# Batch 0 of a sketched attention reworked (token-major k, z from k kᵀ, squares as features), and W1 three waves ahead of W2 at the end

## The chip, the core and the metric

One core of a Trainium2 chip runs the kernel. Its engines have a queue of instructions each and wait for one another by semaphores: TensorE (PE; its weight loads are shown apart as PEld), VectorE (DVE), ScalarE (ACT), GpSimd (POOL), and SyncE (SP), which here only issues DMAs. The metric is the time of one execution on the device in microseconds (us). A profile gives one execution with the start and length of each instruction.

## What is computed

```
a = S1 x,  b = S2 x              # x is a row of q or k (32 numbers), S1 and S2 are 8 x 32
phi(x)[8 i + j] = a[i] b[j]      # 64 features of a row
kv  = sum over tokens of phi(k)^T v          # 64 x 32, for each batch and head
z   = sum over tokens of phi(k)              # 64
x   = (phi(q) kv) / (phi(q) z + 1e-6)        # heads side by side: 128 numbers per token
h   = x w_in                                 # 128 -> 2048
out = (h / (1 + exp(-beta h))) w_out         # 2048 -> 128
```

There are 4 batches, 4 heads and 1088 tokens in a batch, so 4352 tokens reach the second half. All arrays are float32. The kernel folds beta into w_in (winp) and 1/beta into w_out (woutp), both in float16, so that a plain Silu stands between the two products.

## The kernel before

The order of the work on all five engines is written out by hand. Tokens lie across partitions by head: partition 32h + i of a loaded tile holds 34 consecutive tokens of head h. A transpose on VectorE turns 32x32 blocks.

The second half runs in *waves*. `w1` (L320) multiplies up to 512 tokens of xT by two 128-column blocks of winp into one of two PSUM buffers called wave (two banks each), and ScalarE takes the Silu of 1024 columns into g (L338). `w2` (L297) multiplies g by woutp and accumulates over sixteen blocks in the one buffer moeout; after the last block VectorE transposes it into o_sb (L314), which SP stores. Tokens are cut as 256, 256, seven times 512, and 256: 68 waves. In the first, second and last cut a wave is four blocks of 256 tokens. `first` issues a W1 if its tokens are there, `second` issues the oldest outstanding W2, and `rest` (L355) runs what is left when the attention is done: W2 of the wave before goes ahead of the next W1.

The other PSUM buffers are "two" (two banks) and "one" (one bank), a single buffer each, so whoever takes one waits until its last reader is done.

Batch 0 stands in straight code ahead of the waves (L656 to L708). k is transposed (`turn_k`), projected by S1 and S2 with features on partitions (`kps`) and transposed back (`kab`). `gram` multiplies the projections to get z (with `gram_terms` and `gram_z`), `outer` forms phi(k) on VectorE, `kv` sums phi(k)ᵀ v on PE. For q, `spread` makes a and b for all 64 features on partitions, `asb` copies a to SBUF on ScalarE, `mult` multiplies b by it; `den0`, `invert`, `spread_rc`, `num0` and `divide0` write xT. The first 512 tokens go in this stage, the other 576 in the waves' stage. `beta_half` spreads beta over the partitions by two matmuls and a copy, POOL makes winp in eight pieces, and ScalarE makes woutp in sixteen.

From there on one list of names, SEQ (L807), gives the order in which the steps are issued. W and V are `first` and `second`. For batch 1: tk1, kp1, ka1 transpose, project and transpose back k; tq1, qp1, qa1 do it for q; o and O are `outer` for k on POOL and on VectorE, p and P for q; t1n transposes phi(q); Z1 sums phi(k); va1 and vb1 are `kv`; np1, nz1, d1, i1, n1, x10, x11 make z, kv, the denominators, their inverses, the numerators and xT. For the rest of batch 0 they are aB, c0, c1, bB, mB, dB, iB, nB, xB.

Loads are issued on SP in the order k0, q0 (first part), v0, half of w_in, half of w_out, q0 (rest), k1, the other halves, q1, v1, k2, q2, v2; beta and S2 on ACT's queue, S1 and beta_jp on POOL's. Thirteen matmuls on constants run at the start and four before the first W1 (`keep_warm`).

Of the kernel before, what the change touches and what calls it, by code (L numbers as in the profile page):

```python
# [14 lines left out]
P = 128  # L15
# [3 lines left out]
def kernel(  # L19
# [31 lines left out]
    q_chk = [(0, 8), (16, 9)]  # L51
    QW = 32 * 9

# [3 lines left out]
    WARM0 = 13  # L57

    tok_chk = [(0, 256), (256, 256)]
    tok_chk += [(o, min(TCH, NTOK - o)) for o in range(512, NTOK, TCH)]  # L60
# [7 lines left out]
    pso = ctx.enter_context(tc.tile_pool(name="pso", bufs=1, space=bass.MemoryType.PSUM))  # L68
    ps2 = ctx.enter_context(tc.tile_pool(name="ps2", bufs=1, space=bass.MemoryType.PSUM))
    ps1 = ctx.enter_context(tc.tile_pool(name="ps1", bufs=1, space=bass.MemoryType.PSUM))  # L70
# [16 lines left out]
    def cut(t, ap, extra=0):  # L87
# [6 lines left out]
    w_out_sb = sb([P, NJ, P], F32, "w_out_sb")  # L94
    idle = sb([P, P], F16, "idle")
    nc.vector.memset(idle, 1.0)  # L96
    nc.scalar.dma_start(
        out=bass.AP(
            tensor=beta4.tensor,
            offset=beta4.offset,  # L100
            ap=[[32 * beta4.ap[0][0], 4], [1, DFF // 4]],
        ),
        in_=moe_beta.rearrange("(r c) -> r c", r=4),
    )
    sr = []
    for n, (s_, eng) in enumerate(((S1, nc.gpsimd), (S2, nc.scalar))):
        t = sb([P, D], F32, f"sr{n}")
        eng.dma_start(
            out=t, in_=bass.AP(tensor=s_.tensor, offset=s_.offset, ap=[[0, P // R], [D, R], [1, D]])
        )  # L110
        sr.append(t)
    nc.gpsimd.dma_start(out=beta_jp, in_=moe_beta.rearrange("(j p) -> j p", p=P))
    k_t, q_t, v_t = {}, {}, {}

    def load_rows(src, dst, b, tag, parts=((0, T),)):
        if b not in dst:
            dst[b] = ld.tile([P, T, D], F32, tag=tag, name=tag)
# [9 lines left out]


    def load_v(b):
        t = v_t[b] = ld.tile([P, H, NJK, D], F32, tag="v", name="v")  # L130
        if b < B - 1:
            for h in range(H):
                nc.sync.dma_start(
                    out=t[:, h],
                    in_=bass.AP(
                        tensor=v.tensor, offset=v[b, h].offset, ap=[[NJK * D, 4], [T * D, 32], [1, NJK * D]]
                    ),
                )
            return
# [14 lines left out]

    def load_wout(j0, j1):
        nc.sync.dma_start(
            out=w_out_sb[:, j0:j1, :],
            in_=moe_w_out[j0 * P : j1 * P, :].rearrange("(j p) m -> p j m", p=P),
        )

    K_PARTS = ((0, 18), (18, T))
    QA0 = 2 * q_chk[0][1]
    load_rows(k, k_t, 0, "k", K_PARTS)
    load_rows(q, q_t, 0, "q", ((0, QA0),))
    load_v(0)
    load_win(0, DFF // 2)
    load_wout(0, NJ // 2)
    load_rows(q, q_t, 0, "q", ((QA0, T),))
    load_rows(k, k_t, 1, "k")
    load_win(DFF // 2, DFF)  # L170
    load_wout(NJ // 2, NJ)
    load_rows(q, q_t, 1, "q")
# [6 lines left out]
    def keep_warm(n):  # L179
        t = pso.tile([P, TCH], F32, tag="moeout", name="warm")  # L180
        for _ in range(n):
            nc.tensor.matmul(out=t, lhsT=idle, rhs=cut(idle, [[0, 4], [1, P]]), start=True, stop=True)  # L182

    ones = sb([P, P], F32, "ones")
# [3 lines left out]
    ident = sb([P, P], F32, "ident")  # L188
    make_identity(nc, ident)

    hm = sb([P, 2, R], F32, "hm")
    nc.vector.memset(hm, 0.0)
    for h in range(H):
        nc.vector.memset(hm[32 * h : 32 * h + 32, h % 2, :], 1.0)
    gm = sb([P, 4], F32, "gm")
    nc.vector.memset(gm, 0.0)
    for c in range(4):
        nc.vector.memset(gm[32 * c : 32 * c + 32, c : c + 1], 1.0)
    e3 = sb([P, 3], F32, "e3")
    nc.vector.memset(e3, 0.0)  # L200
    nc.vector.memset(e3[:, 1:2], 1.0)

    mk = sb([P, H, R], F32, "mk")
    nc.gpsimd.tensor_tensor(
        out=mk,
        in0=cut(ident, [[2 * R, H], [1, R]]),
        in1=cut(ident, [[2 * R, H], [1, R]], 64),
        op=mybir.AluOpType.add,
    )

    kT2, qT2 = [], []
    for n in range(2):
        qT2.append(sb([P, T, 32], F32, f"qT{n}"))
# [106 lines left out]
    def w1():  # L320
# [22 lines left out]
        if j0 + jn == NJ:  # L343
            moe["ci"] += 1
            moe["w"] = 0
# [502 lines left out]
```

## Time and profile before

| | |
|---|---|
| median of three runs | 116.13 us (115.93 to 116.38) |
| span of the profiled execution, first to last instruction | 113.9 us |
| mean granted TensorE clock | 0.967 |
| PE, DVE, ACT, POOL busy | 100.8, 74.2, 79.2, 28.8 us |
| Silu, L338 | 68 x 1022 ns |
| W1, L329, and W2, L304 | 160 matmuls each |
| first write into xT done | 19.54 us |
| kv of batch 1 begins on PE | 35.5 us |
| last W2 done | 109.9 us |

The profile's own time is its span of 113.9 us; the device time of a run is taken around the whole execution and is about 2.2 us more. Busy PE time is modelled and overlaps, so "busy" is not peak. A float32 matmul appears as two records, and each has a weight load. The granted clock is the share of its full clock that TensorE was allowed.

### The profile page before, as it was taken

The numbers are of one execution on the slowest core, as the hardware profiler recorded it, in microseconds if no ns is written. First come the engines' busy times: TensorE is split into PE (matmuls) and PEld (weight loads), VectorE is DVE, ScalarE is ACT, GpSimd is POOL, SyncE is SP. The second block draws the span as 40 slices with busy tenths as digits, with TensorE's granted clock in tenths as the row PEclk, the third lists the DMA queues.
The fourth block names the chain that finished last, engine by engine and source line by source line (L and its number), as shares of the span: only waits on it lengthen the run. The fifth ranks groups of instructions, "written<-read, shape, count | busy, mean of one in ns | idle before, by whom it ended". The sixth has DMA issues, their size and how long they took to land.

```text
span 113.9 us, 2875 instructions
## 1 busy us (share of the span) xinstructions
PE 100.8 (89%) x1169; PEld 48.3 (42%) x1169; DVE 74.2 (65%) x133; ACT 79.2 (70%) x100; POOL 28.8 (25%) x40
## 2 busy tenths in 40 slices
PE   6969998877999999999999999999998899799840
PEld 2235463323784533435553343465343333334620
DVE  3386828596999799899998899999587001100210
ACT  1426157959879853898996469999926889898830
POOL 6500082807970000530840035065000000000000
PEclk9999558999999999999999999999999999999998
DMA  3679998287234200038502462300320500140323
GB/s 101 233 170 268 307 348 289 106 245 210 103 104 115 53 17 0 3 60 214 211 5 36 75 182 45 53 0 0 60 38 0 84 9 0 26 66 9 50 42 46
DMA packets 24436, 11.33 MB, mean 100 GB/s; under 512 B 18756, under 2 KB 22884, under 8 KB 24424
## 3 DMA queue, kind: packets, MB, share of 16 engines
q1 hardware_dynamic: 23664, 11.05, 37.3%
q8 instruction: 9, 0.15, 0.6%
q10 hardware_dynamic: 696, 0.09, 0.5%
q0 software_dynamic: 64, 0.02, 0.1%
q14 instruction: 3, 0.02, 0.1%
HBM read 8.93 MB, written 2.23 MB: 98 GB/s over the span
## 4 chain that ended last, share of the span: by engine, by line
PE 70%; ACT 12%; DVE 7%; DMA 3%; issue 2%; ACTq 1%; POOL 0%; DVEq 0%
PE moeout L304 24%; PE wave L329 22%; ACT g L338 11%; PE kvz L476 5%; DMA sr<-in_S_dram 3%; PE dps L622 3%; PE betaps L246 3%; PE nps L636 3%; DVE o_sb L314 2%; PE kps L392 2%; PE ndps L545 2%; PE bps L452 1%; DVE xT L647 1%; PE nps L580 1%; PE qps L392 1%
## 5 line engine op out<-in xcount | busy, mean ns | idle before, releaser
L338 ACT ACTIVATE g<-wave 128x1024 f16<-128x1024 f32 x68 | 66.2, 1022 | 18.3 <-PE wave L329 18.3
L304 PE MATMUL moeout<-g,woutp 128*128 128x512 f16 (+1 forms) x160 | 37.8, 347 | 3.5 <-ACT g L338 2.3
L329 PE MATMUL wave<-xT,winp 128*128 128x512 f16 (+1 forms) x160 | 39.7, 347 | 1.2 <-ACT g L338 1.1
L304 PEld LDWEIGHTS <-woutp 128*128 128x128 f16 x160 | 14.9, 97 | 20.8 <-issue 7.8
L329 PEld LDWEIGHTS <-winp 128*128 128x128 f16 x160 | 14.8, 97 | 17.6 <-issue 6.3
L314 DVE STREAM_TRANSPOSE o_sb<-moeout 128x512 f32<-128x512 f32 (+1 forms) x10 | 6.3, 627 | 21.4 <-PE moeout L304 21.2
L428 POOL TENSOR_TENSOR qo<-qab 128x512 f32<-128x512 f32 (+1 forms) x8 | 12.1, 1539 | 10.7 <-DVE qab L413 10.7
L428 POOL TENSOR_TENSOR kp<-kab 128x512 f32<-128x512 f32 (+1 forms) x6 | 7.2, 1216 | 25.7 <-PE wave L329 22.6
L439 DVE STREAM_TRANSPOSE qt<-qo 128x512 f32<-128x512 f32 (+1 forms) x12 | 8.7, 750 | 0.0
L428 DVE TENSOR_TENSOR kp<-kab 128x512 f32<-128x512 f32 (+2 forms) x10 | 8.6, 883 | 0.0
L476 PEld LDWEIGHTS kvz<-kp,v 128*32 128x32 f32 x288 | 5.3, 125 | 4.1 <-issue 3.7
L476 PE MATMUL kvz<-kp,v 128*32 128x64 f32 x288 | 6.4, 244 | 0.0
L182 PE MATMUL warm<-idle 128*128 128x512 f16 x17 | 5.5, 481 | 1.1 <-DVE idle L96 1.1
L256 POOL TENSOR_TENSOR winp<-w_in_sb,beta_bc 128x256 f16<-128x256 f32 x8 | 5.6, 728 | 2.7 <-DMA w_in_sb<-in_moe_w_in_dram 2.7
L365 DVE STREAM_TRANSPOSE kT<-k 128x1088 f32<-128x1088 f32 (+2 forms) x5 | 5.3, 1057 | 1.2 <-DMA k<-in_k_dram 1.2
L572 DVE STREAM_TRANSPOSE rb<-rc 128x576 f32<-128x576 f32 (+1 forms) x9 | 5.9, 685 | 0.2
L271 ACT ACTIVATE woutp<-w_out_sb,rbeta 128x128 f16<-128x128 f32 x16 | 5.1, 394 | 1.1 <-DMA w_out_sb<-in_moe_w_out_dram 1.1
L562 DVE STREAM_TRANSPOSE dT<-dps 128x288 f32<-128x288 f32 (+1 forms) x5 | 2.4, 474 | 4.4 <-PE dps L551 2.4
L371 DVE STREAM_TRANSPOSE qT<-q 128x1088 f32<-128x1088 f32 (+2 forms) x5 | 5.2, 1049 | 0.0
L647 DVE TENSOR_TENSOR xT<-nps,rb 128x576 f16<-128x576 f32 x6 | 4.5, 744 | 0.6 <-PE nps L636 0.3
L392 PE MATMUL kps<-kT,sk 64*32 64x288 f32 x64 | 3.1, 415 | 1.9 <-DVE qp L469 1.0
L428 DVE TENSOR_TENSOR qo<-qab 128x512 f32<-128x512 f32 x4 | 4.8, 1234 | 0.1
(75 smaller groups left out, 77.6 us busy)
## 6 DMA issues: line engine op xcount, KB each, us to landing
v<-in_v_dram SPq DMA_DIRECT2D x15, 144.0 KB
k<-in_k_dram SPq DMA_DIRECT2D x3, 544.0 KB, 8.6
q<-in_q_dram SPq DMA_DIRECT2D x3, 544.0 KB
w_in_sb<-in_moe_w_in_dram SPq DMA_DIRECT2D x2, 512.0 KB
w_out_sb<-in_moe_w_out_dram SPq DMA_DIRECT2D x2, 512.0 KB
out_dram<-o_sb SPq DMA_DIRECT2D x16, 64.0 KB, 2.0
out_dram<-o_sb SPq DMA_DIRECT2D x10, 32.0 KB, 5.6
k<-in_k_dram SPq DMA_DIRECT2D x1, 288.0 KB
```

What stands on the lines that cost most here:

```text
L182: nc.tensor.matmul(out=t, lhsT=idle, rhs=cut(idle, [[0, 4], [1, P]]), start=True, stop=True)
L256: (eng or nc.gpsimd).tensor_tensor(out=winp[:, c0:c1], in0=w_in_sb[:, c0:c1], in1=beta_bc[:, c0:c1], op=MUL)
L304: nc.tensor.matmul(out=moe["acc"][:, :tw], lhsT=woutp[:, j, :], rhs=g[jj], start=(j == 0), stop=(j == NJ - 1),)
L314: nc.vector.transpose(out=o_sb[:, :nt, :].rearrange("p t d -> p (t d)"), in_=moe["acc"][:, :tw])
L329: nc.tensor.matmul(out=wv[:, jj // per, o : o + tw], lhsT=winp[:, (j0 + jj) * P : (j0 + jj + 1) * P], rhs=xT[:, t0 : t0 + tw], start=True, ...
L338: nc.scalar.activation(out=g[:, :, :gw], in_=wv[:, :, :gw], func=ACTF.Silu)
L392: nc.tensor.matmul(out=t[32 * g : 32 * g + 32, pi, :JW], lhsT=skc[rows, :], rhs=moving(rows, g), start=True, stop=True,)
L428: (eng or nc.vector).tensor_tensor(out=cut(dst[b][:, j0:j1], [[F, n], [R, R], [1, R]]), in0=cut(a0, [[2 * R, n], [1, R], [0, R]]), in1=cut ...
L439: nc.vector.transpose(out=QT[b][:, j0:j1].rearrange("p j h c s -> p (j h c s)"), in_=QO[b][:, j0:j1].rearrange("p j h f -> p (j h f)"),)
L476: nc.tensor.matmul(out=KVZ[b][32 * h : 32 * h + 32, :F], lhsT=v_t[b][:, h, j, :], rhs=KP[b][:, j, h, :], start=(j == 0), stop=(j == NJK - ...
L572: nc.vector.transpose(out=rb, in_=cut(rc, [[1, n * tn], [0, 32]], i * tn))
L647: nc.vector.tensor_tensor(out=cut(x0, [[32 * (QB[2 * i + 1] - QB[2 * i]), 2], [1, JW]]), in0=t[:, :, :JW], in1=rb, op=MUL,)
```

## The change

The kernel after differs in three places.

*Batch 0, k.* k0 is loaded in two pieces of tokens j = 0..4 and 5..8 of each group of nine, padded to 36. `kab0` multiplies transposed k as the stationary operand by a block-diagonal S, which gives token-major projections at once; ScalarE copies them and `outer0` multiplies PSUM by the copy on VectorE, or copy by copy on POOL. z comes from k kᵀ: `kk` sums k kᵀ over tokens on PE (68 matmuls), `kk_s2` multiplies by S2, `z_terms` by S1, `z_sum` sums and spreads.

*Batch 0, q.* 4 a b = (a + b)² - (a - b)². `spread_sq` makes the 64 sums and 64 differences of a head for 256 tokens in one matmul, ScalarE squares them (`square`), and z and kv carry the factors 1/4 and -1/4. The first 256 tokens are finished ahead of the first wave; the next 256 are steps dA, iA, nA, xA in SEQ after the first W; the last 576 go as before. S1 is loaded on ACT's queue and S2 on SP's between the two k pieces. v is loaded by token group for all batches (32 partitions a piece, all heads), with a POOL memset before each. Half of beta is spread by DMA, and POOL makes the first half of winp; the second half is a product on VectorE from PSUM (bC, wC0, wC1). woutp is made in four products, two on VectorE (w0, w1) and two on POOL (u2, u3). There are five warming matmuls.

*The end.* The first 512 tokens are one cut, with their first four waves of 256 tokens; the last cut of 256 tokens has eight waves of two blocks, so there are 72 waves. `rest` issues W1 first and W2 when three waves are outstanding, and odd cuts there accumulate in the buffer "one".

```diff
-    WARM0 = 13
-
-    tok_chk = [(0, 256), (256, 256)]
-    tok_chk += [(o, min(TCH, NTOK - o)) for o in range(512, NTOK, TCH)]
+    WARM0 = 5
...
-    K_PARTS = ((0, 18), (18, T))
-    QA0 = 2 * q_chk[0][1]
-    load_rows(k, k_t, 0, "k", K_PARTS)
-    load_rows(q, q_t, 0, "q", ((0, QA0),))
+    load_k0(0, NJ0)
+    load_s(1, S2, nc.sync)
+    load_k0(NJ0, NJK)
+    load_rows(q, q_t, 0, "q", ((0, NA),))
     load_v(0)
-    load_win(0, DFF // 2)
+    load_win(0, DFF // 4)
+    load_beta(0, 512)
+    load_win(DFF // 4, DFF // 2)
+    load_beta(512, 1024)
     load_wout(0, NJ // 2)
-    load_rows(q, q_t, 0, "q", ((QA0, T),))
-    load_rows(k, k_t, 1, "k")
+    load_rows(q, q_t, 0, "q", ((NA, T),))
     load_win(DFF // 2, DFF)
     load_wout(NJ // 2, NJ)
+    load_rows(k, k_t, 1, "k")
     load_rows(q, q_t, 1, "q")
     load_v(1)
...
+    def spread_s():
+        t = bank(2, "srep")
+        nc.tensor.matmul(
+            out=t[:, : 2 * R],
+            lhsT=s12.rearrange("p h d -> p (h d)"),
+            rhs=ident[: 2 * R, : 2 * R],
+            is_transpose=True,
+            start=True,
+            stop=True,
+        )
+        nc.scalar.copy(out=st.rearrange("p n r -> p (n r)"), in_=t[:, : 2 * R])
+        ADD, SUB = mybir.AluOpType.add, mybir.AluOpType.subtract
+        nc.gpsimd.tensor_tensor(
+            out=sbd, in0=cut(st, [[0, H], [1, 2 * R]]), in1=cut(gm, [[1, H], [0, 2 * R]]), op=MUL
+        )
+        for n, op in enumerate((ADD, SUB)):
+            nc.gpsimd.tensor_tensor(
+                out=spm[:, n], in0=cut(st, [[1, R], [0, R]]), in1=cut(st, [[0, R], [1, R]], R), op=op
+            )
...
+    def prep_wout(j0, j1, eng):
+        scaled.update(range(j0, j1))
+        eng.tensor_tensor(
+            out=woutp[:, j0:j1, :],
+            in0=w_out_sb[:, j0:j1, :],
+            in1=cut(rbeta[:, j0:j1], [[1, j1 - j0], [0, P]]),
+            op=MUL,
         )
...
+    waves = []
+    for ci, (t0, tw) in enumerate(tok_chk):
+        if ci == 0:
+            lst = [(0, 256, 0, 4), (0, 256, 4, 4), (256, 256, 0, 4), (256, 256, 4, 4)]
+            lst += [(0, TCH, j, 2) for j in range(8, NJ, 2)]
+        else:
+            lst = [(0, tw, j, 2) for j in range(0, NJ, 2)]
+        for n, (o, w, j0, jn) in enumerate(lst):
+            waves.append((ci, t0, o, w, j0, jn, n == 0, n == len(lst) - 1))
...
+    def w2(wave, g):
+        ci, t0, o, w, j0, jn, head, tail = wave
+        tw = tok_chk[ci][1]
+        if head:
+            if moe["free"] and ci % 2:
+                moe["acc"] = ps1.tile([P, TCH], F32, tag="one", name="moeout1")
+            else:
+                moe["acc"] = pso.tile([P, TCH], F32, tag="moeout", name="moeout")
...
             nc.tensor.matmul(
-                out=moe["acc"][:, :tw],
-                lhsT=woutp[:, j, :],
+                out=moe["acc"][:, o : o + w],
+                lhsT=woutp[:, j0 + jj, :],
                 rhs=g[jj],
-                start=(j == 0),
-                stop=(j == NJ - 1),
+                start=head and jj == 0,
+                stop=tail and jj == jn - 1,
+                skip_group_check=True,
             )
...
     def rest():
-        while moe["ci"] < len(tok_chk):
-            if len(moe["todo"]) >= 2:
+        moe["free"] = True
+        while moe["w"] < len(waves):
+            w1()
+            if len(moe["todo"]) >= 3:
                 second()
-            w1()
         while moe["todo"]:
             second()
...
+    def kk(pairs, n0):
+        if n0 == 0:
+            PS["kk"] = [wave2("kk") for _ in range(2)]
+        for n, t in enumerate(pairs, n0):
+            c = 64 * (n % 2)
+            for h in range(H):
+                x = k_t[0][32 * h : 32 * h + 32, t : t + 2].rearrange("p t d -> p (t d)")
+                nc.tensor.matmul(
+                    out=PS["kk"][h // 2][c : c + 64, h % 2, : 2 * D],
+                    lhsT=x,
+                    rhs=x,
+                    start=(n < 2),
+                    stop=(n >= T // 2 - 2),
+                    skip_group_check=True,
+                )
...
+    def kk_s2():
+        PS["u"] = t = bank(2, "u")
+        for m in range(2):
+            for h in range(H):
+                nc.tensor.matmul(
+                    out=t[32 * h : 32 * h + 32, :R],
+                    lhsT=PS["kks"][:, h, m, :],
+                    rhs=sk[:, m, 1, :],
+                    start=(m == 0),
+                    stop=(m == 1),
+                    skip_group_check=True,
...
+    def z_terms():
+        PS["zt"] = t = sb([P, 2 * R, R], F32, "zt")
         nc.vector.tensor_tensor(
...
+            out=t, in0=cut(PS["u"], [[0, 2 * R], [1, R]]), in1=cut(s1pm, [[1, 2 * R], [0, R]]), op=MUL
+        )
...
+    def z_sum():
+        t = bank(2, "zq_ps")
+        nc.tensor.matmul(
+            out=t[:, :P],
+            lhsT=PS["zt"].rearrange("p c r -> p (c r)"),
+            rhs=cut(gm, [[1, H], [0, 32]]),
+            start=True,
+            stop=True,
+        )
+        nc.scalar.copy(out=zq.rearrange("p h c -> p (h c)"), in_=t[:, :P])
...
+    def kab0(j0, j1):
+        if 0 not in KAB:
+            KAB[0] = sbA.tile([P, NJK, H, 2 * R], F32, tag="kab", name="kab")
+        t = PS["kab", j0 // NJ0] = bank(j0 // NJ0, "kab0")
+        for j in range(j0, j1):
             for c in range(2):
...
+                    out=t[64 * c : 64 * c + 64, 64 * (j - j0) : 64 * (j - j0) + 64],
+                    lhsT=kT0[:, j, 2 * c : 2 * c + 2].rearrange("p g s -> p (g s)"),
+                    rhs=sbd.rearrange("p h c -> p (h c)"),
                     start=True,
                     stop=True,
                 )
-        nc.scalar.copy(out=cut(zb0, [[32, H], [1, 2]]), in_=cut(t, [[2, H], [1, 2]]))
+        nc.scalar.copy(
+            out=KAB[0][:, j0:j1].rearrange("p j h c -> p (j h c)"), in_=t[:, : 64 * (j1 - j0)]
+        )
...
+    def outer0(j0, j1, eng=None):
+        f = None
+        if eng is None:
+            n = j0 // NJ0
+            f = PS["kab", n][:, 64 * (j0 - NJ0 * n) :]
+        outer(KP, 0, KAB, "kp", j0, j1, eng=eng, first=f)
...
+    def spread_sq(i):
+        PS["sq", i] = t = [wave2("sq") for _ in range(2)]
+        for h in range(H):
+            rows = slice(32 * h, 32 * h + 32)
+            nc.tensor.matmul(
+                out=t[h // 2][:, h % 2, :HA],
+                lhsT=spm[rows].rearrange("p m i j -> p (m i j)"),
+                rhs=qT2[0][rows, 8 * i : 8 * i + 8, :],
+                start=True,
+                stop=True,
+            )
+
+    def square(i, pr):
+        nc.scalar.activation(
+            out=SQ[:, 2 * pr : 2 * pr + 2, HA * i : HA * i + HA], in_=PS["sq", i][pr][:, :, :HA], func=ACTF.Square
+        )
...
+    def sq_mm(dst, w, i):
+        for h in range(H):
+            nc.tensor.matmul(
+                out=dst[32 * h : 32 * h + 32, :HA],
+                lhsT=w[:, 32 * h : 32 * h + 32],
+                rhs=SQ[:, h, HA * i : HA * i + HA],
+                start=True,
+                stop=True,
+            )
...
+        PS["kvd"] = t = sb([P, 2, F], F32, "kvd0")
+        nc.vector.tensor_tensor(
+            out=t, in0=cut(KVZ[0], [[0, 2], [1, F]]), in1=cut(pm, [[1, 2], [0, F]]), op=MUL
+        )
...
+    def nd_0():
+        t = bank(1, "ndps")
+        turn_nd(PS["kvd"].rearrange("p c f -> p (c f)"), t[:, :P])
+        nc.scalar.copy(out=ndq, in_=t[:, :P])
...
+    PRE = """
+        S ga ta tb ja jb gb E02 gc u e71 tq e41 e22 s0 e81 zt q00 q01 zs k02 k23 w0 E52 k52 w2 k72 dn
+        kd w3 s1 w1 nd nm q11 iv x cl q10 nB sf rb
+    """
...
+    def den_A():
+        PS["dps"] = t = one("dps")
+        sq_mm(t, zq_, 1)
...
+    def inv_A():
+        RB["A"] = spread_rc(invert(PS["dps"], 1, 8), 0, 8, 1)
...
+    def beta_C():
+        PS["beta"] = t = two("betaps")
+        for n in range(2):
+            beta_mm(2 + n, t[:, n])
+
+    def win_C(n):
+        prep_win(1024 + 512 * n, 1536 + 512 * n, PS["beta"][:, n], nc.vector)
...
-        w3 tk1 w2 w1 W aB c1 V c0 bB mB1 w4 mB0 kp1 w5 ka1 W dB o11 w6 w7 W o10 W tq1 qp1 W qa1
-        O13 nB V W p12 V iB V W W p13 p10 V t12 xB V O12 p11 V t13 W V Z1 W t10 W va1 V W V vb1
-        W W np1 t11 V nz1 d1 W n1 tk2 V i1 V x10 W kp2 x11 W W ka2 V V tq2 V W O21 W o20 V V O22
...
+        W dA iA nA xA W w0 V qB bC wC0 wC1 aB c1 W u2 w1 c0 bB mB1 W V mB0 V tk1 kp1 W ka1 W V dB u3
+        o11 o10 V W tq1 qp1 qa1 o13 W nB p12 iB V V W V W p13 p10 V t12 xB V O12 p11 V t13 W Z1 W t10 W
+        va1 V W V vb1 W W np1 t11 V nz1 d1 W n1 tk2 V i1 V x10 W kp2 x11 W W ka2 V V tq2 V W O21 W o20
```

## The prediction

> **What bounds the kernel now.** I read the chain of work that ended last first, then windows for the clock, then the timeline of the end. The chain names four stages: a head, until VectorE writes the first tokens of xT (19.54 us); a ramp, until PE starts the key-value sums of batch 1 (35.56); a body, until about 86.5; and a tail of W1, Silu and W2 alone.
>
> The chain in the head, in order of time (start, length, what):
>
> ```profile
> 1.88 3.96 DMA sr<-in_S_dram
> ...
> 6.42 0.98 PE kps L392 x16
> ...
> 8.42 1.13 PE betaps L246 x4
> 9.55 0.70 PE gram L490 x18
> ...
> 10.87 1.00 PE zc L512 x16
> 11.86 2.00 PE betaps L246 x4
> 13.87 1.44 PE kvz L476 x48
> ...
> 18.01 0.67 PE nps L580 x16
> ```
>
> It waits for S2, and from 6.42 on it is TensorE. The same betaps work costs 1.13 us at 8.42 and 2.00 at 11.86. The windows say why (after the span, busy us of PE, PEld, DVE, ACT and POOL, granted clock, DMA share, GB/s):
>
> ```profile
> 5.00:6.00 1.00, 0.48 (x3) 0.00 (x0) 0.27 (x3) 0.24 (x1) 0.22 (x1) 1.00 0.28 88
> 9.00:10.00 1.00, 1.00 (x21) 0.52 (x18) 0.36 (x1) 0.66 (x2) 0.00 (x0) 1.00 0.95 266
> 11.00:12.00 1.00, 1.00 (x18) 0.98 (x20) 1.00 (x2) 0.03 (x1) 0.00 (x0) 0.50 0.86 204
> 16.00:17.00 1.00, 0.80 (x28) 0.56 (x20) 0.74 (x2) 0.83 (x3) 1.00 (x2) 0.50 0.98 329
> 18.00:19.00 1.00, 0.99 (x18) 0.40 (x19) 0.68 (x3) 1.00 (x4) 0.00 (x0) 1.00 1.00 364
> 55.00:60.00 5.00, 5.00 (x63) 2.65 (x61) 5.00 (x9) 4.62 (x6) 3.21 (x3) 1.00 0.15 55
> ```
>
> From about 10.9 to 17.6 the clock was half, although PE had just been busy. In the body (last line) PE has no idle time, so what reaches the body late stays late.
>
> The tail, from the timeline (start, us, engine, what, and in brackets the idle time before it):
>
> ```profile
> 98.36 1.94 ACT L338 ACTIVATE g<-wave 128x1024 f16<-128x1024 f32 x2 [0.39 <-PE wave L329]
> ...
> 99.43 0.59 PE L304 MATMUL moeout<-g,woutp 128*128 128x512 f16 x2 [0.31 <-ACT g L338]
> 99.86 0.59 PE L329 MATMUL wave<-xT,winp 128*128 128x512 f16 x2
> 100.35 0.59 PE L304 MATMUL moeout<-g,woutp 128*128 128x512 f16 x2
> 100.55 1.94 ACT L338 ACTIVATE g<-wave 128x1024 f16<-128x1024 f32 x2 [0.26 <-PE wave L329]
> ```
>
> Two waves take 2.2 us, but two Silus back to back only 1.94 - 1.02 + 0.92 = 1.84: W2 of a wave stands on PE ahead of the W1 that refills ScalarE.
>
> **The head.** Full-clock and half-clock prices come from this trace. A record here is half a float32 matmul. Records with 32-column weights: kvz 72 in 1.14 us (16 ns) at full clock, 48 in 1.44 (30 ns) at half. With 64-column weights on 128 rows: gram 39 ns, zc 62 ns. A group of 256 columns: 0.65, at half 1.08 (dps). A transpose: 0.3, at half 0.47 (ndps).
>
> The start is S2, now second on SP's queue. The first k piece landed 2.4 us after its issue, the S pieces 3.6 after theirs; S2's issue should end near 1.7, so 4.1 to 5.3, and I take the middle, 4.7. That passes POOL's three new v memsets (0.31 each) and the identity; its two beta DMAs (0.69 and 0.51 to issue) end before st is copied.
>
> Then the path runs down PE's queue, in order, full/half: S transpose 0.15/0.25; k k^T, 136 records, 2.15/4.1; token-major k, 36 records, 1.4/2.2; two copies of it on ACT 0.6; u 0.3/0.5; squares' features 0.6/1.1; z 0.3/0.4; kvz 1.2/2.15; den 0.6/1.1; features of the second half 0.5/0.9; transpose 0.3/0.45; its copy 0.35; num 0.65/1.05; divide 0.45. Sums 9.55 and 15.6. VectorE's and POOL's outer products (four pieces on POOL, 3.2 us) hide beside it. So the first xT comes at 14.3 or at 20.3. Half of this stretch was at half clock before, and now 5 warming matmuls instead of 13 end at 3.2, with nothing until S arrives, and the k k^T records use a quarter of the rows each. I take the midpoint, 17.3; ends 13.7 (S at 4.1, full) and 20.9. The removed betaps (3.13), gram, zc and the four warm matmuls (0.97) are in the 19.54 that this replaces.
>
> By the Trainium skill, page "TensorE: Matmul & The Clock Gate", section "Why this matters for your kernels", PE must be kept busy for some 4 us to reach the full clock, and only gaps over about 3 us lose it. Five warming matmuls would by that rule be too few, which speaks against the change; but the busy stretch from 4.7 would be at full clock from about 8 on, a head of some 15.8. The row at 11.00 disagrees with its second half: the clock fell with no such gap.
>
> **The ramp.** Time zero is the first xT. Before, xT for tokens 512 to 1087 was written 13.3 us later and kvz began at 16.0. Now, at full clock:
> W1 0.05 to 0.6; den of the second 256 tokens until 1.15 (0.65); VectorE inverts: transpose 0.45, add 0.2, reciprocal 0.25, spread 0.42, until 2.6; divide until 3.0. W2 needs woutp, now a VectorE product of 128x512 (0.7, row qp 0.68) behind that: 3.75. W2, and behind it in PE's queue the betaps (1.13): 5.45. VectorE's two winp products 1.4: 6.85. They hold the buffer "two", so aps waits for them: 7.65. ScalarE copies one half (0.64), then must take the Silu of the W1 in between (1.0) before the other half (0.64): 9.9. bps 10.7, two products 12.25 (1.45), the k transpose of batch 1 13.5 (1.27; PE, with kps at its head, waits from 12.0). kps 14.3, two W1, two W2 and dps in PE's order, a W1, and q's projection at 17.7 (k's and q's transposes hide here). qab 18.6 (0.85), inverse 20.4 (1.8), output transpose 0.7, qt 0.65, divide 0.72: 22.8. That is 9.5 us more than 13.3. Outer product, qt and three waves as before: kvz at 25.0 instead of 16.0.
>
> Of the 9.0, PE work is only 2.4 (dps and nps of the second half 1.3, betaps 1.13); VectorE gets 4.0 more and the rest is waits in series. ScalarE loses sixteen scalings (0.39 each), but only 1.16 us of them stood on the chain. The unknown prices are the four woutp and winp products on VectorE: 0.62 to 1.24 each by the outer products' rows without and with POOL beside them, so -0.3 to +2.2 together. I take 0.7, as winp reads PSUM like qp. If the clock also falls here (before, the ramp had PE 3.66 of 5 us busy at its emptiest, 20 to 25; now a third to two thirds), PE's dense stretch from 13.5 to 17 doubles: +3.5.
>
> **Loads.** k of batch 1 now follows w_in and w_out on SP, about 1 MB later; at the 329 GB/s of the 16.00 row that is 3 us. Before, it was read at 20.15 without a wait; now at 17.3 + 12.25 = 29.5. Nothing, unless the ramp shrinks by some 7 us. v's new shape matters to nobody's wait on the chain.
>
> **The body** keeps its order: 78.4 us from kvz to the end before.
>
> **The tail.** W2 now follows a wave later, so after a Silu W1 is next: 0.43 + 0.2 of PE beside another Silu of 0.92. Both need 0.87 (PE, four matmuls) and 0.92 (ACT) per wave; ScalarE binds. Before, 20 waves took from 87.16 to 109.24. Now 16 x 0.92 and 8 half waves at 0.92 - 512 x 0.83 ns = 0.50 (copies of 1024 and 512 columns: 1.01, 0.59): 18.7, starting 0.45 earlier (three W2 ahead instead of four), and the last W2 is 0.25 shorter. 109.24 becomes 105.5, together 4.0. The chain's three output transposes (0.73 each) fall out except the first, which W1 ahead should cover; ends 3.0 and 4.0, taken 3.8.
>
> **Sum.** 17.3 + 25.0 + 78.4 - 3.8 = 116.9 of span, against 113.9. The median of three runs, 116.13, is 2.2 above the span of this execution, so 119.1.
>
> **Rivals.**
> Full clock throughout the head: S at 4.1 and every row at its full price puts xT at 13.7, and the total at 13.7 + 25.0 + 78.4 - 4.0 + 2.2 = 115.3, faster by 0.7%. It decides below a head of 14.1 with this ramp. For it: the clock was full from 4 to 10.9 before with similar gaps. Against it: the fall at 10.9 after projections of 64 rows.
> Half clock in the ramp: 119.1 + 3.5 = 122.6. For it: waits of 1 to 2 us in series on PE; against it, 20 to 25 before was full at 73% busy.
> The tail doesn't run ahead (PE at 0.87 is close to 0.92, and a W2 that waits for the first output transpose blocks the W1 behind it): 3.8 less gain, 122.9. Against it: only one such wait is left.
>
> **How the numbers follow.** The likeliest: slower by a ramp that loses more than head and tail win, 0.45, with its own range 117.3 to 121.3 (head 15.5 to 19.5). Half clock in the ramp 0.23, no lead in the tail 0.05: all slower, with the likeliest 0.73. Head at full clock 0.27: by its bounds on VectorE's prices, 0.16 faster (under 115.55) and 0.11 within 0.5%, which is about what this kernel's runs can tell. The range 115.1 to 122.8 leaves out about 0.1 on each side.
>
> **What would show it.** Head: the first divide into xT near 17, a clock of 0.5 in part of 7 to 15. Ramp: 22 to 23 us from it to the divide of tokens 512 on; aps waiting for winp on VectorE, bps for ScalarE's copy, kps for the transpose. Tail: Silus without idle time, 0.92 apart. I am wrong if the divide comes before 14.5, or if the ramp's waits overlap so that kvz of batch 1 starts before 37.

## The result and the profile after

| | before | after |
|---|---|---|
| median, runs of the first comparison | 116.25 us (115.93 to 117.36, 4) | 122.83 us (121.08 to 124.25, 4) |
| ratio | | 1.048 [1.035, 1.061] |
| the profiled execution: time, span | 116.13, 113.9 us | 124.25, 122.5 us |
| PE busy | 100.8 us | 107.0 us |

The change made the kernel slower by about 5 %. The ratio compares the faster runs of each alone (of after 121.08 and 122.23), since two of its four are over 1.5 % longer; the medians of all runs are 5.7 % apart. The profiled execution of after is the longest of its four; a second profile, taken below on another chip, has the same span with the half clock at fewer places, and the two are read together.

The chain of work that ended last, after, in the head (start, length, what):

```profile
1.74 4.60 DMA k<-in_k_dram
...
6.36 0.72 DVE kT L804
...
7.13 1.12 PE kab L615 x16
...
12.39 2.08 PE kvz L534 x72
...
17.46 0.43 DVE xT L841
```

and in the ramp:

```profile
21.13 0.78 DVE woutp L318
...
21.96 0.61 PE moeout L366 x4
22.57 1.08 PE betaps L293 x4
...
23.68 1.30 DVE winp L300 x2
...
25.02 0.74 PE aps L510 x14
...
26.61 1.03 ACT g L398
...
27.77 1.34 PE bps L510 x16
...
29.20 1.42 DVE qp L527 x2
30.62 1.23 DVE kTs L423
...
31.99 1.03 PE kps L450 x16
...
39.93 0.72 DVE o_sb L377
40.65 0.59 DVE qt L497
41.24 0.65 DVE xT L738
```

The chain changes engine at nearly every step: PE waits for VectorE, VectorE for PE, once for a Silu. Windows of after, as those shown of before (after the span, busy us of PE, PEld, DVE, ACT and POOL, then granted clock, DMA share, GB/s):

```profile
11.00:12.00 1.00, 1.00 (x10) 0.41 (x2) 0.51 (x1) 0.30 (x1) 1.00 (x2) 1.00 1.11 330
...
30.00:31.00 1.00, 1.00 (x7) 0.73 (x5) 1.00 (x2) 0.95 (x1) 0.00 (x0) 0.50 0.14 42
44.00:45.00 1.00, 1.00 (x18) 0.36 (x20) 0.96 (x2) 0.76 (x2) 0.00 (x0) 0.50 0.06 16
...
55.00:60.00 5.00, 4.88 (x46) 1.95 (x35) 4.53 (x8) 2.96 (x3) 1.63 (x2) 1.00 0.00 0
```

The granted clock halves in the ramp and again where the key-value sums of batch 1 run; at 55 it is full and PE has next to no idle time (4.88 of 5 us busy), as before. In the tail ScalarE now runs nearly without a break (timeline of after; in brackets the idle time before):

```profile
98.55 2.85 ACT L398 ACTIVATE g<-wave 128x1024 f16<-128x1024 f32 x3 [0.89 <-PE wave L389]
101.67 16.53 ACT L398 ACTIVATE g<-wave 128x1024 f16<-128x1024 f32 x21 [0.27 <-PE wave L389]
```

By stages, from the two profiles:

| stage | before | predicted | after | change |
|---|---|---|---|---|
| start to first xT | 19.54 | 17.3 | 17.88 | -1.7 |
| ramp, to kv of batch 1 | 16.0 | 25.0 | 26.8 | +10.8 |
| body, to the last numerators | 48.8 | 48.8 | 51.4 | +2.6 |
| tail, to the end of the span | 29.6 | 25.8 | 26.5 | -3.1 |
| span | 113.9 | 116.9 | 122.5 | +8.6 |

### The profile page after: what moved, and what is told of

It reads as the page before. It is cut to its first block, busy times and chain, and to the rows that moved or that the text cites. A ratio compares the mean times of both kernels' runs of the same rounds, so it can differ in the third digit from the quotient of the medians.

```text
span 122.5 us, 3095 instructions
## 1 busy us (share of the span) xinstructions
PE 107.0 (87%) x1270; PEld 50.9 (42%) x1270; DVE 73.4 (60%) x137; ACT 74.4 (61%) x90; POOL 34.1 (28%) x51
## 4 chain that ended last, share of the span: by engine, by line
PE 63%; DVE 15%; DMA 8%; SPq 4%; issue 3%; ACT 3%; DVEq 0%; ACTq 0%
PE wave L389 21%; PE moeout L366 18%; PE kvz L534 6%; DMA out_dram<-o_sb 4%; DMA k<-in_k_dram 4%; SPq L346 3%; PE dps L768 3%; DVE o_sb L377 3%; ACT g L398 3%; PE nps L782 3%; DVE rb L718 2%; PE sq L639 2%; PE kps L450 1%; PE ndps L686 1%; DVE xT L793 1%
## 5 line engine op out<-in xcount | busy, mean ns | idle before, releaser
L398 ACT ACTIVATE g<-wave 128x1024 f16<-128x1024 f32 (+1 forms) x72 | 66.4, 985 | 26.7 <-PE wave L389 26.3
L389 PE MATMUL wave<-xT,winp 128*128 128x512 f16 (+1 forms) x152 | 41.6, 369 | 3.6 <-DVE xT L738 2.0
L366 PE MATMUL moeout<-g,woutp 128*128 128x512 f16 (+1 forms) x152 | 40.2, 371 | 1.4 <-DVE woutp L318 1.0
L389 PEld LDWEIGHTS <-winp 128*128 128x128 f16 x152 | 13.9, 99 | 24.5 <-issue 13.8
L486 POOL TENSOR_TENSOR kp<-kab 128x512 f32<-128x512 f32 (+2 forms) x11 | 11.4, 1067 | 39.5 <-PE wave L389 20.5
L366 PEld LDWEIGHTS <-woutp 128*128 128x128 f16 x152 | 14.7, 101 | 18.1 <-issue 4.3
L486 DVE TENSOR_TENSOR kp<-kab 128x512 f32<-128x512 f32 x5 | 4.9, 1004 | 0.0
L782 PE MATMUL nps<-qt,nd 32*32 32x288 f32 x192 | 4.8, 412 | 0.0
L423 DVE STREAM_TRANSPOSE kTs<-k 128x1088 f32<-128x1088 f32 x3 | 3.9, 1292 | 0.0
L768 PE MATMUL dps<-qt,zbg 128*32 128x288 f32 x48 | 3.5, 411 | 0.3 <-DVE nd L763 0.3
L677 DVE TENSOR_TENSOR z<-kp 128x1024 f32<-128x1024 f32 x3 | 3.6, 1209 | 0.2
L527 DVE TENSOR_TENSOR qp<-bps,asb 128x576 f32<-128x576 f32 x2 | 1.4, 752 | 3.6 <-PE bps L510 3.6
## 6 DMA issues: line engine op xcount, KB each, us to landing
k<-in_k_dram SPq DMA_DIRECT2D x3, 544.0 KB, 11.2
```

What stands on the lines that cost most here:

```text
L366: nc.tensor.matmul(out=moe["acc"][:, o : o + w], lhsT=woutp[:, j0 + jj, :], rhs=g[jj], start=head and jj == 0, stop=tail and jj == jn - 1, ...
L389: nc.tensor.matmul(out=wv[:, jj // per, c : c + w], lhsT=winp[:, (j0 + jj) * P : (j0 + jj + 1) * P], rhs=xT[:, t0 + o : t0 + o + w], start ...
L398: nc.scalar.activation(out=g[:, :, :gw], in_=wv[:, :, :gw], func=ACTF.Silu)
L486: (eng or nc.vector).tensor_tensor(out=cut(dst[b][:, j0:j1], [[F, n], [R, R], [1, R]]), in0=cut(a0 if first is None else first, [[2 * R, n ...
L768: nc.tensor.matmul(out=dps[32 * h : 32 * h + 32, :JW], lhsT=zbg[b % 2][:, h, fc, :], rhs=QT[b][:, :, h, fc, :], start=(fc == 0), stop=(fc ...
L782: nc.tensor.matmul(out=tiles[g // 2][32 * h : 32 * h + 32, g % 2, :JW], lhsT=ND[b][rows, fc, 32 * h : 32 * h + 32], rhs=QT[b][rows, :, h, ...
```

## The experiments

Each stands beside runs of the kernel before on the same chip; a ratio is to those.

### e1: the tail alone

The kernel before with only the new `rest` and the second accumulator. The last cut keeps its four waves of four blocks.

```diff
-            if len(moe["todo"]) >= 2:
-                second()
             w1()
+            if len(moe["todo"]) >= 3:
+                second()
...
+            if moe["free"] and ci % 2:
+                moe["acc"] = ps1.tile([P, TCH], F32, tag="one", name="moeout1")
```

> The kernel before with only the end changed: W1 first, W2 when three waves are outstanding, odd cuts in a second accumulator (the last cut keeps its four waves of four blocks). If the end is a gain by itself, as the forecast has it (3.0 to 4.0, and 3.0 between the two profiles' tails): 112.3 to 113.3 us, Silus 0.92 apart. If the lead only helps a kernel whose waves come late: within 1 us of 116.2.

112.02 us (111.22 to 113.61), ratio 0.964 [0.949, 0.978]. It beats both kernels and is the best version of this study. In its timeline ScalarE has no idle time in twenty Silus:

```profile
87.03 18.44 ACT L341 ACTIVATE g<-wave 128x1024 f16<-128x1024 f32 x20 [0.87 <-PE wave L332]
105.52 0.60 PE L307 MATMUL moeout<-g,woutp 128*128 128x256 f16 x4 [0.32 <-ACT g L341]
```

From the last numerators (84.50) to the end is 25.6 us; it was 29.6. So the third part of the change is worth 4.0 us by itself, and the first two must have cost what the whole lost, and this on top.

### e6: the lead without the second accumulator

As e1, but without the last two lines of its diff.

> The kernel before with W1 three waves ahead of W2 at the end, but one accumulator. Theory, the lead carries the tail's gain and the second accumulator next to nothing, since an output transpose of 0.73 us fits under the Silu of a wave that is already in PSUM: 112.0 to 112.9. Rival, the W2 that waits for the transpose blocks the W1 behind it, three times 0.4 to 0.7: 113.2 to 114.2.

113.92 us (113.36 to 114.44), ratio 0.986 [0.978, 0.993]: where the rival put it. Its tail takes 26.7 us, so the lead is worth 2.9 of the 4.0 and the accumulator 1.1. Its timeline of ScalarE shows where:

```profile
88.29 2.86 ACT L338 ACTIVATE g<-wave 128x1024 f16<-128x1024 f32 x3 [0.87 <-PE wave L329]
91.41 7.44 ACT L338 ACTIVATE g<-wave 128x1024 f16<-128x1024 f32 x8 [0.27 <-PE wave L329]
99.11 7.44 ACT L338 ACTIVATE g<-wave 128x1024 f16<-128x1024 f32 x8 [0.25 <-PE wave L329]
106.81 1.02 ACT L338 ACTIVATE g<-wave 128x1024 f16<-128x1024 f32 x1 [0.27 <-PE wave L329]
```

At each change of cut the W2 at the head of PE's queue waits for the output transpose (0.72 us); PE idles 0.32 to 0.34 there, and 0.25 to 0.27 passes through to ScalarE. Of the 1.9 us between the medians of e6 and e1 (2.5 by the two ratios) the tail is 1.1; the rest lies ahead of it, where e6, on another chip, had a mean clock of 0.945 against 0.969.

### e2: the order of the ramp

The changed kernel with the first line of the ramp's list in another order: q's transpose, betaps and k's transpose sooner, the first W2 and woutp after aps and its copies.

```diff
-        W dA iA nA xA W w0 V qB bC wC0 wC1 aB c1 W u2 w1 c0 bB mB1 W V mB0 V tk1 kp1 W ka1 W V dB u3
+        W qB dA bC iA nA xA W wC0 wC1 aB tk1 c1 c0 w0 W V bB w1 W u2 mB1 mB0 V kp1 V W ka1 W V dB u3
```

> The changed kernel with another order in the ramp only: q's second transpose first, the betaps and both winp products ahead of the woutp product, the transpose of k of batch 1 where VectorE would wait for bps, both copies of aps together; same instructions. If the ramp's loss is waits in series: by the forecast's steps kps comes at 8.7 us after the first xT instead of 14.3, so 5 to 6 us less than the changed kernel, 116 to 117.5. If it is the half clock in ramp and body (26 to 33 and 43 to 50 us in its profile), the order alone gives at most 2 us: 120 or more.

118.79 us (118.02 to 119.31), ratio 1.028 [1.016, 1.039]. Between the expectations. The ramp went from 26.8 to 21.6 us with no work taken out, but not all of that is order: this profile's granted clock is 1.00 throughout, and of the 26.8 some 1.2 are half clock (bps, kps and a W1, see the ramp below). That leaves about 4 us for the order; the ratios (1.028, against 1.048 and 1.071 for the unedited kernel) say 2 to 4 %. What is left shows in its timeline of VectorE and PE:

```profile
24.20 1.31 DVE L423 STREAM_TRANSPOSE kTs<-k 128x1088 f32<-128x1088 f32 x1 [0.40 <-DMA k<-in_k_dram]
...
33.33 0.85 DVE L471 STREAM_TRANSPOSE qab<-qps 128x288 f32<-128x288 f32 x2 [2.04 <-PE qps L450]
34.10 0.44 DVE L703 STREAM_TRANSPOSE dT<-dps 128x288 f32<-128x288 f32 x1
```

```profile
38.48 1.02 PE L389 MATMUL wave<-xT,winp 128*128 128x512 f16 x4 [2.04 <-DVE xT L738]
```

VectorE idles for 2.04 us before qab while the denominators (done at 31.6) wait behind it, and PE runs out of tokens for 2.04 us before the divide. The chain of this run names the load of k of batch 1 for 11.6 us; the idle time says that it was late by 0.40.

### e5: the divide first

As e2, with denominators, inverse and divide ahead of q's transpose and projection.

```diff
-        W qB dA bC iA nA xA W wC0 wC1 aB tk1 c1 c0 w0 W V bB w1 W u2 mB1 mB0 V kp1 V W ka1 W V dB u3
-        o11 o10 V W tq1 qp1 qa1 o13 W nB p12 iB V V W V W p13 p10 V t12 xB V O12 p11 V t13 W Z1 W t10 W
+        W qB dA bC iA nA xA W wC0 wC1 aB tk1 c1 c0 w0 W V bB w1 W u2 mB1 mB0 V kp1 V W dB ka1 iB V nB u3
+        W xB o11 o10 tq1 V W qp1 V qa1 o13 W V p12 W V W V p13 p10 V t12 W V O12 p11 V t13 W Z1 W t10
```

> The reordered ramp of the second run, with the denominators, their inverses and the divide of tokens 512 on put ahead of the transposes and projection of q of batch 1 (there, the divide stood behind qab, o_sb and qt on VectorE, and PE had no more tokens from 36.4 to 38.5). Theory, waits in series on VectorE: from the durations of that run the products with bps end at 29.0, denominators 29.8, inverse 32.4, divide 33.1 instead of 38.4; PE's idle time there (2.0 and 0.7 us before waves) goes, so 115.0 to 116.4. Rival, PE work itself carries what is left of the loss: 118 to 119.5, with an early divide and the same time.

130.45 us (129.78 to 132.69), ratio 1.127 [1.117, 1.137]. Both theories missed. The divide did come at 33.4, as planned, 5 us sooner than in e2, and the time is 12 us longer. Timeline of PE (the sums of batch 1 begin in the last line, in e2 at 40.8):

```profile
34.80 0.72 PE L450 MATMUL qps<-qT,sk 64*32 64x288 f32 x16 [2.38 <-DVE qT L429]
...
41.07 0.59 PE L366 MATMUL moeout<-g,woutp 128*128 128x512 f16 x2 [0.47 <-ACT g L398]
...
43.27 0.59 PE L366 MATMUL moeout<-g,woutp 128*128 128x512 f16 x2 [1.17 <-ACT g L398]
...
45.98 0.77 PE L534 MATMUL kvz<-kp,v 128*32 128x64 f32 x40
```

and windows of the body, 54 us each, first e5, then e2:

```profile
46.00:100.00 54.00, 46.91 (x621) 20.63 (x624) 40.35 (x61) 35.19 (x39) 12.30 (x9) 1.00 0.25 52
```

```profile
40.80:94.80 54.00, 53.20 (x720) 24.27 (x720) 47.34 (x74) 41.23 (x45) 12.29 (x9) 1.00 0.25 53
```

Between the two profiles (spans 130.9 and 116.2 us) e5 is 5.0 ahead at the divide and 14.7 behind at the end. Of these 19.7 us 10.2 go up to the sums of batch 1: there stand the steps of q that the divide has overtaken, PE waits 2.38 for q's transpose, and the clock is half from 36.2 to 39.6. The body takes 56.3 us to the last numerators, against 49.0 in e2, and the tail 28.6 against 26.4.

What the body lost can be counted in the list. A W whose tokens are not there and a V with nothing outstanding are skipped. In after and e2 three V and two W around the late divide are skipped, and W1 builds up its lead behind it. In e5 the tokens were there sooner: these V took waves that had only just been issued, and two W ahead of the divide of batch 1 found no tokens left. From there on the lead is one to two waves smaller through the whole body: a W2 stands on PE right behind the Silu that it needs, as it does for 1.17 us at 43.27 already. From 46 on such waits come to 3.3 us, and W1 waits 4.1 for the divides; e2 has neither. That the smaller lead is the cause is argued from this count and these waits. In e9, which keeps the lead, the body takes 51.3 us, but e9 differs in more than the lead.

### e8: woutp on ScalarE, in the order of e5

```diff
-        W qB dA bC iA nA xA W wC0 wC1 aB tk1 c1 c0 w0 W V bB w1 W u2
+        W qB dA bC iA nA xA a0 W wC0 wC1 aB tk1 c1 c0 W V bB a1 W u2
```

Here a0 and a1 scale four blocks of 128 columns each on ScalarE, as the kernel before does.

> The order of e5 with the two woutp products (0.6 to 0.8 us each on VectorE) moved back to ScalarE as eight scalings of 128 columns (0.31 each in the kernel before), four in ScalarE's idle time ahead of the second Silu. Theory, VectorE's added products are waits of the ramp: the first W2 no longer waits for woutp, bps comes about 1 us sooner, and the time is 0.8 to 1.5 us below e5. Rival, they lie beside other waits (or the scalings delay the copies of aps by as much): within 0.5 us of e5.

130.98 us (127.98 to 131.58). It carries the lost lead of e5, and tells nothing on woutp.

### e9: the inverse early, the lead kept

As e2, with one move (iB ahead of qp1, xB right behind nB), and W and V placed so that three waves are outstanding at va1.

```diff
-        o11 o10 V W tq1 qp1 qa1 o13 W nB p12 iB V V W V W p13 p10 V t12 xB V O12 p11 V t13 W Z1 W t10 W
+        o11 o10 V W tq1 iB qp1 qa1 o13 W nB xB p12 V W p13 p10 V t12 V O12 p11 t13 W Z1 W t10
```

> The reordered ramp of the second run with one thing more: the inverses of tokens 512 on stand ahead of the projection of q of batch 1, the divide right behind the numerators, and W1 and W2 are placed so that three waves are outstanding at the key-value sums of batch 1 as there (the run that put the divide first had lost one to two of them for the whole body). Theory, order of the waits: VectorE's idle 2.04 us at 31.3 takes the inverse, the divide comes at 36.2 instead of 38.4, PE's idle 2.0 there goes, and the time is 116.0 to 117.3, ratio to before about 1.005 to 1.015. Rival, the loss left in that run is PE's own added work: 118.3 to 119.5, no change against it.

117.25 us median against 116.73. The four runs are 114.80, 116.99, 117.51 and 118.48, with mean granted clocks of 1.0, 0.983, 0.985 and 0.971: the same code, nearly in the order of its clock. The median lies in the range of the theory, but the runs lie too far apart to tell more. In the run at full clock it is faster than any run of the kernel before beside it (116.13 to 117.39).

### e10: e9 with woutp on ScalarE

> As e9, with the two woutp products of VectorE moved back to ScalarE as eight scalings of 128 columns (0.31 each). Theory, these products are waits of the ramp: in the second run PE idled 1.01 before the first W2 for woutp with bps queued behind it, so bps, the divide and the end come 0.8 to 1.2 sooner than in e9. Rival, they lie beside other waits: within 0.4 of e9.

115.52 us (114.61 to 116.77), ratio 0.987 [0.979, 0.995]: all that the change computes, in another order and with one piece of work put back on its old engine, is faster than the kernel before. It is so by the tail: e1, which has the tail alone, stands at 0.964 (on another chip), so the new head and ramp still cost some 2 % in this order. The divide is done 16.6 us after the first xT (19.3 in e2, 24.0 in after). PE's timeline, e9 first (this profile has half clock here), then e10:

```profile
25.46 1.03 PE L366 MATMUL moeout<-g,woutp 128*128 128x256 f16 x4 [1.52 <-DVE woutp L318]
26.43 1.26 PE L510 MATMUL bps<-qT,s 32*64 32x288 f32 x16
```

```profile
24.03 0.60 PE L373 MATMUL moeout<-g,woutp 128*128 128x256 f16 x4
25.10 0.74 PE L517 MATMUL bps<-qT,s 32*64 32x288 f32 x16 [0.47 <-issue]
```

The wait for woutp is gone, and bps no longer stands behind it. Whether that is worth the 0.8 to 1.2 expected stays open: the medians differ by 1.7, but e9's one run at full clock (114.80) lies within the runs of e10. Nor is the wait in e9's profile that of woutp alone: VectorE, with woutp next in its queue, idled there for 1.86 us until k of batch 1 had landed:

```profile
23.52 1.31 DVE L423 STREAM_TRANSPOSE kTs<-k 128x1088 f32<-128x1088 f32 x1 [1.86 <-DMA k<-in_k_dram]
```

Part of what e10 gained ahead of the divide comes back behind it. Its body takes 51.3 us (49.0 in e2); PE now waits for VectorE's sum of phi(k):

```profile
42.04 0.32 PE L671 MATMUL kvz<-zs,ones 128*32 128x64 f32 x8 [1.33 <-DVE zs L688]
```

### e3: constant matmuls in the gaps of the ramp

25 matmuls on constants, six ahead of wC0, five ahead of bps, six ahead of kps, eight ahead of the first batch's last W1s; nothing is left out.

```diff
-        W dA iA nA xA W w0 V qB bC wC0 wC1 aB c1 W u2 w1 c0 bB mB1 W V mB0 V tk1 kp1 W ka1 W V dB u3
+        W dA iA nA xA W w0 V qB bC f6 wC0 wC1 aB c1 W u2 w1 f5 c0 bB mB1 W V mB0 V f6 tk1 kp1 W ka1 W V dB u3
...
-        V O12 p11 V t13 W Z1
+        V O12 p11 V f8 t13 W Z1
```

> The changed kernel with 25 matmuls on constants, put where PE waited in the ramp (6 before aps, 5 before bps, 6 before kps, 8 before the waves of batch 0's last tokens); their result is not used. If the half clock carries the loss: it stays full from 17 us on, ramp 24 to 25 instead of 26.8, body 48.8 instead of 51.4, total 3 to 4.5 us less, 117.5 to 119. If the waits carry it: at most 2 us less (119.8 or more), with the divide of tokens 512 on still 22 us or more after the first.

121.16 us (120.93 to 124.13), ratio 1.048 [1.037, 1.059]. Three of the four runs had a clock of 0.992 to 0.996 and took 120.9 to 121.4. So with the clock nearly full the loss is still 5 %, which speaks for the waits; what the 25 matmuls cost by themselves isn't measured apart. In the fourth run, the profiled one, the clock halved at about 22, ahead of the first of them (six in 2.74 us at 25.7, where six later ones took 1.46), and these six held up aps by 1.3 us.

### e7: the changed kernel again

> The changed kernel once more, without an edit, for a profile at a clock like that of the runs it is compared with. If the clock of 25.9 to 32.6 and 43 to 49.6 in the first profile was no property of the kernel, the ramp from the first xT to the key-value sums of batch 1 takes about 25 to 26 us instead of 26.8, the body 49 instead of 51.4, and the time is 121 to 122.3. If it is one, the same half clock shows at the same places and the time is 122 to 124.

124.04 us (123.14 to 124.52), ratio 1.071 [1.062, 1.081]. By the time, the half clock is a property of the kernel; by the place only the ramp's half is. The windows of this profile:

```profile
23.00:24.00 1.00, 0.57 (x4) 0.31 (x4) 1.00 (x2) 0.00 (x0) 0.00 (x0) 0.94 1.10 245
...
30.00:31.00 1.00, 0.10 (x8) 0.13 (x14) 0.00 (x0) 1.00 (x2) 0.00 (x0) 0.50 0.31 76
...
34.00:35.00 1.00, 0.55 (x4) 0.25 (x2) 0.97 (x1) 0.20 (x1) 0.00 (x0) 0.94 0.02 8
...
47.00:48.00 1.00, 1.00 (x43) 0.76 (x43) 0.97 (x2) 1.00 (x2) 0.00 (x0) 1.00 0.06 16
```

The clock was half from about 24 to 34, the ramp took 28.4 us, and the sums of batch 1 at 47 ran at full clock: the body took 49.0 us, as before. So the 2.6 us of the body in the first profile belong to that execution, and not to the kernel.

### e4 and e11: thirteen warming matmuls, and one

```diff
-    WARM0 = 5
+    WARM0 = 13
```

> The changed kernel with 13 warming matmuls as before. If five were too few and the head ran at half clock because of it: token-major k, squares, z, kvz and den at their full-clock prices, first xT 1.3 us earlier (clock falls again near 11) to 3 us earlier (it holds), at 14.9 to 16.6 instead of 17.9; total 1 to 3 us less. If the late second k piece (landed 6.3) sets the head: within 1 us of the changed kernel.

124.95 us (123.86 to 126.46), ratio 1.079 [1.064, 1.093]: missed. PE's timeline:

```profile
1.06 5.73 PE L193 MATMUL warm<-idle 128*128 128x512 f16 x13 [1.06 <-DVE idle L102]
6.72 0.28 PE L257 MATMUL srep<-ident,s 16*128 16x16 f32 x1
6.93 0.94 PE L555 MATMUL kk<-k 32*64 32x64 f32 x64
...
10.69 0.71 PE L639 MATMUL sq<-qT,spm 32*128 32x256 f32 x8
...
13.83 1.93 PE L534 MATMUL kvz<-kp,v 128*32 128x64 f32 x64 [1.76 <-issue]
```

Behind the longer warming the head runs at full speed (kk 64 in 0.94 instead of 1.29, the squares' features in 0.71 instead of 1.24). But it held back srep from 4.14 to 6.72, kvz stopped for 1.76 us with nothing in the profile that it waited for, and from about 14 the granted clock was half, so that kvz and den cost 3.0 us as in after. The first xT came at 19.3 instead of 17.9.

```diff
-    WARM0 = 5
+    WARM0 = 1
```

> The changed kernel with one warming matmul instead of five. Theory, five never reach the full clock: k times its transpose already runs at half clock in the changed kernel (64 records in 1.29) and the first full-clock shapes come at about 15.5, so the head is the same within 0.5 us and the time 121 to 124, as the changed kernel. Rival, the five count toward the busy time after which the clock rises: the head's shapes stay at half clock about 2 us longer, the first xT comes 1 us later or more, and the time is over 124.

125.69 us (124.23 to 126.95), ratio 1.067 [1.059, 1.076], against 1.071 [1.062, 1.081] of the unedited kernel in e7. The time alone passes the rival's bound of 124, but so did e7; the ratios agree. The head's shapes are the same (kk 1.29, the squares' features 1.24) and the first xT comes at 18.95, against 17.88 and 18.67. So nothing shows here that the other four warming matmuls do.

## Why the prediction was right, and where it was not

The time fell at the upper edge of the range (and beyond it in e7's runs, 124.04): slower, as forecast, by 6.6 us instead of 3. The mechanism was right, a ramp of waits that loses more than head and tail win; some of the numbers came out by luck. The working can be gone through by its terms.

**Head, 17.3: measured 17.88, by another mixture.** S2 landed at 4.1, the early end. I took the midpoint of full and half clock; in fact nearly all of it ran at half speed up to 15, and it came out near the midpoint since k times its transpose cost 2.8 us instead of 4.1 and S2 came 0.6 sooner than taken. That is luck: the midpoint stood for a mixture that did not occur. The squares' features show it in PE's timeline of after:

```profile
10.43 1.24 PE L639 MATMUL sq<-qT,spm 32*128 32x256 f32 x8
...
15.25 0.88 PE L639 MATMUL sq<-qT,spm 32*128 32x256 f32 x8
```

I had left two things out. The second piece of k lands at 6.34, and kab waits for it (0.25). And at full speed the path is longer than the sum of its steps, as e9's profile shows:

```profile
9.74 0.71 PE L639 MATMUL sq<-qT,spm 32*128 32x256 f32 x8
...
13.22 0.99 PE L534 MATMUL kvz<-kp,v 128*32 128x64 f32 x56 [1.94 <-issue]
```

kvz stops there for 1.94 us with nothing in the profile that it waits for, as it does for 1.76 in e4 and 1.15 in e5. So e9's first xT comes at 17.0, although PE is at full speed from about 8 on: the 13.7 of the first rival was out of reach. What kvz waits for stays open.

By the Trainium skill, page "TensorE: Matmul & The Clock Gate", section "Why this matters for your kernels", some 4 us of busy PE bring the full clock; from 4.14 that would be at about 8, by my estimate. In after PE had worked from 4.14 with gaps of 0.25 and 0.35, and the features at 10.43 still took the long time. In e9, with the same five warming matmuls and the same small ones behind them but no gap from 4.38 on, the last 72 records of k times its transpose took 1.08 at 8.01 (1.50 in after) and the features 0.71: as the page has it. In e5, with one gap of 0.21 ahead of 8, they took 0.71 too. So small float32 matmuls can bring the full speed; whether the gaps made the difference in after isn't tested.

**Ramp, 25.0: measured 26.8, nearly step by step as written.** From the first xT: woutp 4.0 (3.75 predicted), betaps 5.8 (5.45), winp 7.1 (6.85), aps 7.9 (7.65), bps 11.2 (10.7), products 12.7 (12.25), k's transpose 14.0 (13.5), kps 15.1 (14.3), q's projection 18.9 (17.7), qab 19.7 (18.6), inverse 22.0 (20.4), divide 24.0 (22.8). The waits are those named: aps for winp, bps for ScalarE (it begins behind the Silu between the two copies, not behind the second copy), kps for the transpose. VectorE's products cost 0.65 to 0.78 each (0.7 taken). My sum has two slips here: its steps from the inverse on give the divide at 22.5, not 22.8, and from the divide to kvz I wrote 2.2 us for "as before", where before had 2.7. They nearly cancel. Of the 1.5 that are then missing at the divide, bps and kps at half clock are 0.8 and a longer inverse 0.5. From the divide to kvz went 2.8 us, in which a W1 of 0.6 took 1.0 at half clock.

**Half clock in the ramp, a rival at 0.23: it came.** All but one of the eight runs of the unedited kernel stood at or above 122. Its price of 3.5 us holds for the second profile, whose ramp is 3.4 longer than forecast, and is too high for the first (1.8, of which some 1.2 are clock), where the half clock ended at 32.6 instead of 34. That it was an addition and not the whole loss is what e3 speaks for, as far as its added matmuls allow: at a clock of 0.99 it still takes 121. So the likeliest case and this rival both happened. That the median, 122.83, lies so near the rival's 122.6 is in part chance: of the 5.6 us by which the first profile's span passes the sum, the ramp has only 1.8, the body 2.6, head and tail the rest.

**"The body keeps its order": right** at full clock (49.0 in e7 against 48.8). The 2.6 us in the first profile are half clock at 43 to 50, which I had only put in the ramp.

**Tail, -3.8: measured -3.1.** The mechanism was right, and e1 gives 4.0. Two terms of after were mis-sized. A half wave's Silu was taken at 0.50 and takes 0.57 (16.53 us for 13 whole ones at 0.92 and eight halves), so that eight halves cost 0.9 more than the four whole Silus of e1. And W1 did not cover the first output transpose in full: ScalarE idles 0.27 there. In after the first new cut of the tail is an even one and takes moeout again, so its W2 waits for the transpose as in e6; in e1, where the cuts are numbered otherwise, it is odd and takes the second accumulator.

**"Loads: nothing": right for after,** where k of batch 1 was read at 30.6. In e2, where it is read at 24.2, the load is late by 0.40, which is near the bound given ("unless the ramp shrinks by some 7 us"). In e9's profile, read at 23.5, it is late by 1.86. So a shorter ramp meets the loads next.

**Of the 9.0 us, "PE work is only 2.4 and the rest is waits in series": shown in the main.** e2 took 5.2 us out of the ramp (about 4 without the clock's part) and e10 7.4 out of the way to the divide (16.6 instead of 24.0; 2.3 of it came back in the body), without taking out any of the work. The size of PE's own part isn't measured; that e10 still costs some 2 % against e1 is of its order. What remains open is how much of e10 is woutp, how much the late load and how much the clock, and why the granted clock halves in one execution and not in another.

## What to carry to other kernels

Measure the parts of a combined change apart: here a tail worth 4 us was hidden under a rework that lost more. Work that moves to another engine takes a place in its queue; walk through the steps in issue order, as the prediction does for the ramp: another order of the same work was worth 2 to 4 % here. When something is moved in a hand-written order, count afterwards how many waves are outstanding at each step: e5 gained 5 us at the divide and lost nearly 20 behind it, half of them in a body and a tail whose instructions nobody had touched.

## What was not expected of the hardware

The granted-clock column does not show every half speed. In after's head it stands at 1.00 while the five warming matmuls start 0.43 us apart (five take 2.32, the single one of e11 0.61) and the squares' features take 1.24 us; the same shape takes 0.71 in the heads of e4, e5 and e9. At the start of a profile, durations of one shape tell more than the column.

The stretches with a granted clock of 0.50 come in steps. In the thirteen profiles (without the end of each span) there are seventeen, and added up from windows of 1 us they last 3.4 us (seven of them), 6.8 (six), 10.2 (three) or 13.7 (one): one to four times 3.41. e7's is an example: ten windows at 0.50, and the two at its ends, at 0.94, give 0.12 us each. Where a profile has more than one, their starts are whole multiples of 3.41 apart too: 25.9 and 43.0 in after (five), 12.3, 22.6, 36.2 and 104.5 in e5 (three, four and twenty). The profiles of e2 and e10 have none. So in these runs the clock changes at ticks 3.41 us apart, and a fall lasts at least one of them. What sets it off was not found: in e4 it fell at 13.8 behind a stop of PE of 1.76 us, in before at 10.8 with no gap over 0.17 in the 3.4 us ahead of it. The four runs of e9 lie between 114.80 us (mean clock 1.0) and 118.48 (0.971) with the same code.
